# Linear attention and a bilinear feed-forward on one core: every matrix product as plain fp32 on four 32-column tiles

## The chip, the core and the metric

The kernel runs on one core of a Trainium2 chip. The core has five engines that run side by side and meet at semaphores: TensorE (PE in the profile; its weight loads are listed apart as PEld), VectorE (DVE), ScalarE (ACT), GpSimd (POOL) and SyncE (SP), whose queue starts most of the transfers. The metric is the device time of one execution in microseconds (us); lower is better.

## What is computed

A linear attention with a complex decay per channel, four batches by eight heads by 768 steps with 48 channels, and then a feed-forward of two products that are multiplied elementwise and a third product. Cut to what matters:

```
scale = np.minimum(mag, 0.999) / (mag + 1e-06)      # mag = |a_re + i a_im|
for t in range(S):                                  # S = 768
    S_re, S_im = (ar * S_re - ai * S_im + k_t v_t^T, ar * S_im + ai * S_re)
    y[:, :, t] = q_t @ S_re
x = y as (3072 tokens, 384)
out = ((x @ w_a) * (x @ w_b)) @ w_out               # d_model 384, d_ff 1536
```

Inputs, weights and result are fp32.

## The kernel before, in words

**Units.** The work is cut into 12 units: two pairs of batches, six chunks of 128 steps each. A unit has 256 tokens (two batches of 128, index `i`) and all eight heads. `prep(u)` makes a unit's decays and scaled queries and keys on DVE and ACT, `stack(u)` copies them into `stk` by DMA, `attn(u)` is the chunked attention, and the feed-forward of unit `u` runs while the attention of unit `u + 1` is made. The loop at the end goes over units `w` and, in each, over the 12 blocks `f` of 128 columns of d_ff: `gemm1` of block `f`, some pieces of `attn(w + 1)` (`slot`), then `gemm2` of the block two earlier (`LAG` is 2).

**Matrix products on PE.** Two sorts stand side by side. The feed-forward is made in fp32r, a reduced form of fp32 that is read in one pass, on all 128 columns of the array: weights, x and the product h are each held as a high part (rounded to fp32r) and a low part (what is left), and each product is made of three: high by high, low by high, high by low. `gemm1` (L549) makes for each of the two halves `m` (w_a and w_b) of a block 3 x 3 matmuls with 256 moving columns (`ab`); ACT and DVE then turn `ab` into `h_t`, `hh` and `hl` (L560 to L563: ACT copy, DVE product, ACT rounding, DVE difference). `gemm2` (L570) makes for each of two token halves three matmuls with 384 moving columns into `o`. The attention is in plain fp32: `scores` (L432, 128 moving columns), `transposes` of keys (L443, PE's transpose, 96 columns), `state` (L499, 48 or 96 moving columns) on all 128 or 96 columns, and `outputs` (L476, into `xp`), which alone is cut into tiles of 32 array columns: four matmuls, one for each quarter of the output's partitions, are issued one behind the other.

**Weights.** They lie in memory as 64-bit pairs. Three DVE operations (L140, L142, L144) turn a block's pairs into fp32 in a scratch tile; ACT rounds it (L148, high part), PE subtracts the high part from it (L153 in fp32, L154 in fp32r, times minus one with `nident`), and ACT copies out the low part (L155). Six blocks are done ahead of the first attention, six during unit 0. In the attention, x gets its low part in `residual` (L484 on DVE; L486 on PE and L489 on ACT for the first two units).

**What sets the order.** Each engine works its instructions off in program order; a scheduler places them by priority when the program is built (`high_priority` moves the evacuations of PSUM forward), and `issue_after` holds pieces of the attention behind a named matmul of the feed-forward.

Of the kernel before, what the change touches and what calls it, by code (L numbers as in the profile page):

```python
# [9 lines left out]
F32R = mybir.dt.float32r  # L10
# [42 lines left out]
CONV_ON_AB = 7  # L53
# [20 lines left out]
def tile_kernel(ctx: ExitStack, tc: tile.TileContext, a_d, qk_d, v_d, w_d, qn_d, kn_d, vn_d, an_d, out_d):  # L74
# [45 lines left out]
    nident = const.tile([128, 128], F32, name="nident")  # L120
    act.mul(out=nident.bitcast(F32R), in_=ident, mul=-1.0)
    w_t = {}
    raws = {}

    def r(ap):
        return ap.bitcast(F32R)

# [6 lines left out]
    def split_weights():  # L134
        for f in range(NF):
            for m, (c0, n) in enumerate(WPART):
# [12 lines left out]
                if f < CONV_ON_AB:  # L149
                    lp = ps_ab.tile([128, 512], F32, name="ab")  # L150
                else:
                    lp = ps_m.tile([128, 512], F32, name="pm")
                pe.matmul(out=lp[:, 0:n], lhsT=ident, rhs=t, start=True, stop=False)  # L153
                pe.matmul(out=lp[:, 0:n], lhsT=r(nident), rhs=r(hi), start=False, stop=True)  # L154
                act.copy(out=r(lo), in_=lp[:, 0:n])  # L155
# [255 lines left out]
    ff_last = [None, None]  # L411

    def attn(u, xh, xl):
# [10 lines left out]
        def scores(i, hg):  # L424
            qs, ks = cols(i)
            sp = ps_m.tile([128, 4, 128], F32, name="pm")
            for h4 in range(4):
                h = hg * 4 + h4
                with ExitStack() as behind:
                    if u >= GATE_FROM and not ams:  # L430
                        behind.enter_context(tc.issue_after(ff_last[0]))
                    pe.matmul(out=sp[:, h4], lhsT=stk[:, h, ks], rhs=stk[:, h, qs], start=True, stop=True)  # L432
# [6 lines left out]
        def transposes(i, hg):  # L439
            qs, ks = cols(i)  # L440
            tp = ps_m.tile([128, 512], F32, name="pm")
            for h4 in range(4):
                pe.transpose(out=tp[:, h4 * KS:(h4 + 1) * KS], in_=stk[0:KS, hg * 4 + h4, ks],  # L443
                             identity=ident[0:KS, 0:KS])
# [6 lines left out]
        def outputs(i, _):  # L451
# [17 lines left out]
            with tc.high_priority(offset=ATTN_FIRST):  # L469
# [8 lines left out]
                act.copy(out=r(xh[:, :, qs]), in_=xp)  # L478

        def residual(i, _):  # L480
            qs, ks = cols(i)
            if u > 1:
                with tc.high_priority(offset=ATTN_FIRST):
                    vec.tensor_tensor(out=r(xl[:, :, qs]), in0=xps[i], in1=xh[:, :, qs], op=ALU.subtract)  # L484
                return
            pe.matmul(out=xps[i], lhsT=r(nident), rhs=r(xh[:, :, qs]), start=False, stop=True,  # L486
                      skip_group_check=True)
            with tc.high_priority(offset=ATTN_FIRST):
                act.copy(out=r(xl[:, :, qs]), in_=xps[i])  # L489

        def state(i, hg):
# [4 lines left out]
            for h4 in range(4):  # L496
                h = hg * 4 + h4
                o = (h // 2) * VG + (h % 2) * (64 if own else 16)
                pe.matmul(out=kp[0:KS, h4 * n:(h4 + 1) * n], lhsT=kt_tiles[u][:, i, h * KS:(h + 1) * KS],  # L499
                          rhs=v_t[:, o:o + n], start=True, stop=True)  # L500
# [3 lines left out]
            with tc.high_priority(offset=ATTN_FIRST):  # L504
# [4 lines left out]
                if rescaled(c):  # L509
# [3 lines left out]
                 (outputs, 0, 0), (scores, 1, 0), (residual, 0, 0), (state, 0, 0), (scores, 1, 1),  # L513
                 (state, 0, 1), (transposes, 1, 0), (transposes, 1, 1), (outputs, 1, 0),
                 (state, 1, 0), (residual, 1, 0), (state, 1, 1)]
        if u >= KT_FROM:
            order = [(scores, 0, 0), (scores, 0, 1), (pause, 0, 0), (outputs, 0, 0), (scores, 1, 0),
                     (residual, 0, 0), (state, 0, 0), (scores, 1, 1), (state, 0, 1), (outputs, 1, 0),
                     (state, 1, 0), (residual, 1, 0), (state, 1, 1)]
        if u == 0:  # L520
            order = [(scores, 0, 0), (scores, 0, 1), (outputs, 0, 0), (scores, 1, 0), (scores, 1, 1),
                     (residual, 0, 0), (outputs, 1, 0), (transposes, 0, 0), (transposes, 0, 1),
                     (residual, 1, 0), (state, 0, 0), (state, 0, 1), (transposes, 1, 0), (transposes, 1, 1),
# [6 lines left out]
    def pieces(u):  # L530
        if u >= KT_FROM:
            return 9 if u % NCH + 1 == NCH else 13
        return 8 if u % NCH + 1 == NCH else 16

    def new_x():
        return (moe.tile([128, NJ, TOK], F32, name="xh"), moe.tile([128, NJ, TOK], F32, name="xl"))


    def w_ab(f, part, blk):
        m, b = divmod(blk, NJ)  # L540
        return w_t[f, m][:, part, b * 128:(b + 1) * 128]

    def gemm1(f, xh, xl, ps_ab=ps_ab, moe=moe, spare=None):
        ab = ps_ab.tile([128, 512], F32, name="ab")
        for m in range(2):
            n = 0
            for i in range(NJ):
                for part, xt in ((0, xh), (0, xl), (1, xh)):
                    ff_last[0] = pe.matmul(out=ab[:, m * TOK:(m + 1) * TOK],  # L549
                              lhsT=r(w_ab(f, part, m * NJ + i)),  # L550
                              rhs=r(xt[:, i, :]), start=n == 0, stop=n == 8).ins
                    n += 1
        if spare and f % 2:
            h_t = spare()[:, 0:TOK]
        else:
            h_t = moe.tile([128, TOK], F32, name="h_t", bufs=1)
        hh = moe.tile([128, TOK], F32, name="hh", bufs=HB)
        hl = moe.tile([128, TOK], F32, name="hl", bufs=HB)
# [286 lines left out]
```

## Time and profile before

| | |
|---|---|
| median of 3 runs | 684.1 us (683.79 to 685.3) |
| the profiled execution's own time | 683.28 us |
| its span, first to last instruction | 681.5 us |
| mean granted TensorE clock | 0.969 of full speed |
| busy: PE, PEld, DVE, ACT, POOL | 639.5, 603.5, 558.1, 334.9, 5.5 us |
| instructions: PE, DVE, ACT | 5778, 1283, 670 |
| moved by DMA | 63.14 MB, 93 GB/s |

The profile has one row for each group of equal instructions: line, engine, operation, tile written and read, shape, count, then the busy time and the mean duration of one. A matmul's form reads as "rows*columns of the array", then what it streams. A plain fp32 matmul shows as two instructions, each with its own weight load (192 products of `scores` are 384 instructions); an fp32r matmul and PE's transpose as one. Matmuls overlap, so a duration in a row is a latency; what one costs in a stream is the distance from its start to the next one's. In the view of the slices, a digit is the busy share of a fortieth of the span in tenths, and PEclk the granted clock in tenths.

### The profile page before, as it was taken

What the parts mean: (1) busy time and instruction counts of PE and PEld (TensorE: products, weight loads), DVE (VectorE), ACT (ScalarE), POOL (GpSimd) and SP (SyncE); (2) the same over time, 40 slices, a digit from 0 to 9 for tenths busy, and PEclk for the clock granted to TensorE, in tenths of its full rate; (3) what the DMA queues carried; (4) which work ended last, traced back from release to release, by engine and by line L of the source; (5) the groups of instructions that cost most, each with busy time, mean ns of one, the idle gap of its engine ahead of it and who ended that gap; (6) DMA issues with size and microseconds to landing.
All of it is one profiled execution on the core that took longest, in us unless ns stands there. A gap on an engine that the chain in (4) does not pass through costs nothing.

```text
span 681.5 us, 14237 instructions
## 1 busy us (share of the span) xinstructions
PE 639.5 (94%) x5778; PEld 603.5 (89%) x5778; DVE 558.1 (82%) x1283; ACT 334.9 (49%) x670; POOL 5.5 (1%) x11
## 2 busy tenths in 40 slices
PE   3547899999999999999999999999999999999996
PEld 1214789999999999999999999999999999999996
DVE  6999899998989989989899899899899898433221
ACT  7347665734545446255363464664573573222321
POOL 3000000000000000000000000000000000000000
PEclk9576899999999999999999999999999999999998
DMA  8983300512415115033151151601511500400000
GB/s 286 395 317 94 120 1 12 176 51 64 124 39 149 57 48 183 16 116 108 29 164 47 38 154 48 166 25 49 148 42 62 154 24 15 119 12 2 24 1 27
DMA packets 52120, 63.14 MB, mean 93 GB/s; under 512 B 28624, under 2 KB 32208, under 8 KB 52048
## 3 DMA queue, kind: packets, MB, share of 16 engines
q1 hardware_dynamic: 48592, 57.45, 28.0%
q10 hardware_dynamic: 3456, 4.72, 1.9%
q8 instruction: 47, 0.77, 0.5%
q14 instruction: 25, 0.20, 0.1%
HBM read 38.54 MB, written 4.72 MB: 63 GB/s over the span
## 4 chain that ended last, share of the span: by engine, by line
PE 53%; DVE 32%; ACT 7%; DMA 3%; issue 3%; SPq 2%; ACTq 0%; DVEq 0%
PE ab L549 27%; PE o L570 13%; PE xp L476 4%; PE pm L432 4%; DVE a_t L300 3%; PE pm L499 3%; DVE qk L320 3%; DVE pr L238 2%; DVE hl L563 2%; DVE am L435 2%; ACT kt L408 2%; DVE z L305 1%; DVE o_sb L142 1%; DVE h_t L561 1%; DVE z L244 1%
## 5 line engine op out<-in xcount | busy, mean ns | idle before, releaser
L549 PE MATMUL ab<-xh,w 128*128 128x256 f32 x1728 | 339.2, 285 | 0.0
L549 PEld LDWEIGHTS ab<-xh,w 128*128 128x128 f32 x1728 | 276.1, 188 | 2.8 <-issue 2.0
L549 PE MATMUL ab<-xl,w 128*128 128x256 f32 x864 | 244.3, 283 | 0.0
L549 PEld LDWEIGHTS ab<-xl,w 128*128 128x128 f32 x864 | 162.8, 188 | 0.5
L570 PE MATMUL o<-w,hh 128*128 128x384 f32 x576 | 153.7, 346 | 0.4 <-ACT o_sb L709 0.4
L570 PEld LDWEIGHTS o<-w,hh 128*128 128x128 f32 x576 | 97.3, 188 | 1.5 <-ACT o_sb L709 0.6
L570 PE MATMUL o<-w,hl 128*128 128x384 f32 x288 | 97.3, 338 | 0.0
L560 ACT COPY h_t<-ab 128x256 f32<-128x256 f32 x75 | 27.6, 368 | 67.5 <-PE ab L549 65.4
L153 PE MATMUL ab<-o_sb,ident 128*128 128x384 f32 x42 | 28.0, 766 | 30.0 <-DVE o_sb L144 30.0
L432 PE MATMUL pm<-stk 128*128 128x128 f32 x384 | 54.6, 281 | 0.6 <-DMA stk<-qk 0.5
L570 PEld LDWEIGHTS o<-w,hl 128*128 128x128 f32 x288 | 54.1, 188 | 0.0
L432 PEld LDWEIGHTS pm<-stk 128*128 128x128 f32 x384 | 50.1, 194 | 4.4 <-issue 2.2
L560 ACT COPY o_sb<-ab 128x256 f32<-128x256 f32 x66 | 24.3, 369 | 59.7 <-PE ab L549 59.1
L561 DVE TENSOR_TENSOR h_t<-ab,h_t 128x256 f32<-128x256 f32 x75 | 31.5, 420 | 26.0 <-ACT h_t L560 25.9
L562 ACT CAST hh<-h_t 128x256 fp32r<-128x256 f32 x75 | 30.1, 402 | 44.2 <-DVE h_t L561 44.1
L561 DVE TENSOR_TENSOR o_sb<-ab,o_sb 128x256 f32<-128x256 f32 x66 | 27.7, 420 | 29.0 <-ACT o_sb L560 29.0
L238 DVE TENSOR_TENSOR pr<-z 128x384 f32<-128x384 f32 (+1 forms) x91 | 47.2, 525 | 2.0
L562 ACT CAST hh<-o_sb 128x256 fp32r<-128x256 f32 x66 | 26.6, 403 | 45.1 <-DVE o_sb L561 44.9
L300 DVE TENSOR_TENSOR a_t<-z,b_t 128x768 f32<-128x768 f32 x48 | 45.1, 954 | 0.0
L153 PEld LDWEIGHTS ab<-o_sb,ident 128*128 128x128 f32 x42 | 9.5, 267 | 39.4 <-DVE o_sb L144 29.6
L320 DVE TENSOR_TENSOR qk<-qk,z 128x768 f32<-128x768 f32 (+1 forms) x34 | 43.5, 1279 | 0.2
L476 PE MATMUL xp<-am,v_t 128*32 128x128 f32 x768 | 37.7, 281 | 2.9 <-DVE am L435 2.8
(117 smaller groups left out, 897.8 us busy)
## 6 DMA issues: line engine op xcount, KB each, us to landing
w<-in_dram SPq DMA_DIRECT2D x36, 384.0 KB, 7.8
qk<-in_dram SPq DMA_DIRECT2D x12, 768.0 KB, 4.8
stk<-qk SPq DMA_DIRECT2D x48, 192.0 KB, 3.3
a_t<-in_dram SPq DMA_DIRECT2D x11, 768.0 KB, 4.5
stk<-qk SPq DMA_DIRECT2D x24, 192.8 KB, 3.3
out_dram<-o_sb ACTq DMA_DIRECT2D x24, 192.0 KB, 1.9
v_t<-in_dram SPq DMA_DIRECT2D x24, 128.0 KB, 2.6
v_t<-in_dram SPq DMA_DIRECT2D x24, 96.0 KB, 3.0
```

What stands on the lines that cost most here:

```text
L153: pe.matmul(out=lp[:, 0:n], lhsT=ident, rhs=t, start=True, stop=False)
L238: vec.tensor_tensor(out=pr[:, :, :, o:o + n], in0=view(zz, W + at_(i) + 2 * o, [[W, 2], [-W, 2], [2, n]]), in1=tok(slice(1, 3), i - 1, o, ...
L300: vec.tensor_tensor(out=pz[:, s].rearrange("p (j b e) -> p j b e", j=SUB // 2, e=2), in0=zb[:, 1 + s], in1=view(bb, (1 + k - s) * NB, [[0, ...
L320: vec.tensor_tensor(out=qk4[:, :, k, x0:x1], in0=qk4[:, :, 1, x0:x1], in1=z[:, k].rearrange("p (j t) -> p j t", j=NJ).unsqueeze(2).broadca ...
L432: pe.matmul(out=sp[:, h4], lhsT=stk[:, h, ks], rhs=stk[:, h, qs], start=True, stop=True)
L476: run = pe.matmul(out=xp[qd * 32:(qd + 1) * 32, ti], lhsT=l, rhs=rr, start=st, stop=sp_, tile_position=(0, qd * 32), skip_group_check=True ...
L499: pe.matmul(out=kp[0:KS, h4 * n:(h4 + 1) * n], lhsT=kt_tiles[u][:, i, h * KS:(h + 1) * KS], rhs=v_t[:, o:o + n], start=True, stop=True)
L549: ff_last[0] = pe.matmul(out=ab[:, m * TOK:(m + 1) * TOK], lhsT=r(w_ab(f, part, m * NJ + i)), rhs=r(xt[:, i, :]), start=n == 0, stop=n == ...
L560: act.copy(out=h_t, in_=ab[:, 0:TOK])
L561: vec.tensor_tensor(out=h_t, in0=ab[:, TOK:2 * TOK], in1=h_t, op=ALU.mult)
L562: ff_last[1] = act.copy(out=r(hh), in_=h_t).ins
L570: ff_last[0] = pe.matmul(out=os_[tt][:, 0:DM], lhsT=r(ht[:, ts]), rhs=r(w_t[f, 2][:, part, :]), start=(f == 0 and n == 0), stop=(f == NF - ...
```

## The change

All matrix products go through one helper, `tiled`, or through `outputs`, whose matmuls are in that form already. The helper cuts the stationary operand into quarters of 32 columns and issues one plain fp32 matmul for each quarter, the last quarter first. The high and low parts of weights, x and h are gone, with what made them: per weight block two ACT copies and two PE matmuls (the third DVE operation now writes the fp32 weight over the front half of the block's own pairs), `residual`, ACT's rounding and DVE's difference of h. Scores, transposes (now a product with the identity) and state go through `tiled` as well. `gemm1` takes 3 products of 256 columns for each half instead of 9, `gemm2` one of 384 columns for each token half instead of 3.

```diff
+    def tiled(out, lhsT, rhs, start=True, stop=True):
+        for qd in reversed(range(lhsT.shape[-1] // 32)):
+            q = slice(qd * 32, (qd + 1) * 32)
+            ff_last[0] = pe.matmul(out=out[q], lhsT=lhsT[:, q], rhs=rhs, start=start, stop=stop,
+                                   tile_position=(0, qd * 32), skip_group_check=True).ins
...
-                vec.scalar_tensor_tensor(out=tu, in0=raw[:, :, 1], scalar=0xC0000000, in1=tu,
+                w = raw.rearrange("p c s -> p (c s)")[:, 0:n]
+                w_t[f, m] = w.bitcast(F32)
+                vec.scalar_tensor_tensor(out=w, in0=raw[:, :, 1], scalar=0xC0000000, in1=tu,
                                          op0=ALU.bitwise_and, op1=ALU.bitwise_or)
-                w_t[f, m] = wpool.tile([128, 2, n], F32, name=f"w{m}{f}")
-                hi, lo = w_t[f, m][:, 0], w_t[f, m][:, 1]
-                act.copy(out=r(hi), in_=t)
...
-                pe.matmul(out=lp[:, 0:n], lhsT=ident, rhs=t, start=True, stop=False)
-                pe.matmul(out=lp[:, 0:n], lhsT=r(nident), rhs=r(hi), start=False, stop=True)
-                act.copy(out=r(lo), in_=lp[:, 0:n])
...
-                    pe.matmul(out=sp[:, h4], lhsT=stk[:, h, ks], rhs=stk[:, h, qs], start=True, stop=True)
+                    tiled(sp[:, h4], stk[:, h, ks], stk[:, h, qs])
...
-                pe.transpose(out=tp[:, h4 * KS:(h4 + 1) * KS], in_=stk[0:KS, hg * 4 + h4, ks],
-                             identity=ident[0:KS, 0:KS])
+                tiled(tp[:, h4 * KS:(h4 + 1) * KS], stk[0:KS, hg * 4 + h4, ks], ident[0:KS, 0:KS])
...
-                act.copy(out=r(xh[:, :, qs]), in_=xp)
-
-        def residual(i, _):
...
+                act.copy(out=x_t[:, :, qs], in_=xp)
...
-                pe.matmul(out=kp[0:KS, h4 * n:(h4 + 1) * n], lhsT=kt_tiles[u][:, i, h * KS:(h + 1) * KS],
-                          rhs=v_t[:, o:o + n], start=True, stop=True)
+                tiled(kp[0:KS, h4 * n:(h4 + 1) * n], kt_tiles[u][:, i, h * KS:(h + 1) * KS], v_t[:, o:o + n])
...
         for m in range(2):
-            n = 0
             for i in range(NJ):
-                for part, xt in ((0, xh), (0, xl), (1, xh)):
-                    ff_last[0] = pe.matmul(out=ab[:, m * TOK:(m + 1) * TOK],
-                              lhsT=r(w_ab(f, part, m * NJ + i)),
-                              rhs=r(xt[:, i, :]), start=n == 0, stop=n == 8).ins
-                    n += 1
...
+                tiled(ab[:, m * TOK:(m + 1) * TOK], w_t[f, m][:, i * 128:(i + 1) * 128], x_t[:, i, :],
+                      i == 0, i == NJ - 1)
+        a_sb = moe.tile([128, TOK], F32, name="a_sb")
+        h_t = moe.tile([128, TOK], F32, name="h_t", bufs=HB)
         with tc.high_priority(offset=MOE_FIRST):
-            act.copy(out=h_t, in_=ab[:, 0:TOK])
-            vec.tensor_tensor(out=h_t, in0=ab[:, TOK:2 * TOK], in1=h_t, op=ALU.mult)
-            ff_last[1] = act.copy(out=r(hh), in_=h_t).ins
-            vec.tensor_tensor(out=r(hl), in0=h_t, in1=hh, op=ALU.subtract)
-        return hh, hl
+            ff_last[1] = act.copy(out=a_sb, in_=ab[:, 0:TOK]).ins
+            vec.tensor_tensor(out=h_t, in0=ab[:, TOK:2 * TOK], in1=a_sb, op=ALU.mult)
+        return h_t
...
-            ts = slice(tt * 128, (tt + 1) * 128)
-            for n, (ht, part) in enumerate(((hh, 0), (hh, 1), (hl, 0))):
-                ff_last[0] = pe.matmul(out=os_[tt][:, 0:DM], lhsT=r(ht[:, ts]), rhs=r(w_t[f, 2][:, part, :]),
-                          start=(f == 0 and n == 0), stop=(f == NF - 1 and n == 2)).ins
+            tiled(os_[tt][:, 0:DM], h_t[:, tt * 128:(tt + 1) * 128], w_t[f, 2], f == 0, f == NF - 1)
```

The lines that drop the `residual` entries from the order of the attention's pieces, adapt the count of pieces and rename arguments are left out of the diff.

What this does to PE's instructions shows in the built programs, where a matmul is one row whatever its passes; a row has the line, the operation, the tile written and the tiles read (with numbers where several exist), the output's shape and a count. First the steady state of the feed-forward, in the middle of unit 2. Before, the second half of `gemm1` of one block and `gemm2` of the block two earlier read:

```order
L549 MATMUL ab<-xh,w_438 128x256
L549 MATMUL ab<-xl,w_438 128x256
L549 MATMUL ab<-xh,w_438 128x256 x2
L549 MATMUL ab<-xl,w_438 128x256
L549 MATMUL ab<-xh,w_438 128x256 x2
L549 MATMUL ab<-xl,w_438 128x256
L549 MATMUL ab<-xh,w_438 128x256
L570 MATMUL o_2258<-w_388,hh 128x384 x2
L570 MATMUL o_2258<-w_388,hl 128x384
L570 MATMUL o_2259<-w_388,hh 128x384 x2
L570 MATMUL o_2259<-w_388,hl 128x384
```

In the changed program, PE's rows at the same place hold both halves of a block, its `gemm2`, and the first half of the next block; every row is now written by the helper (L123):

```order
L123 MATMUL ab<-x_t,w_146 32x256 x12
L123 MATMUL ab<-x_t,w_148 32x256 x12
L123 MATMUL o_2526<-w_130,h_t 32x384 x4
L123 MATMUL o_2527<-w_130,h_t 32x384 x4
L123 MATMUL ab<-x_t,w_152 32x256 x12
```

Nine full-width matmuls of a half have become twelve of a quarter's width, and three of a token half have become four; the sequence of blocks is the same.

Second, a place in unit 2 where pieces of the next unit's attention stand between the blocks: scores (`pm<-stk`), state (`pm<-v_t,kt`) and transposes (`pm<-ident,stk`). Before:

```order
L432 MATMUL pm<-stk 128x128 x4
L499 MATMUL pm<-v_t,kt 96x48 x4
L570 MATMUL o_2258<-w_894,hh 128x384 x2
L570 MATMUL o_2258<-w_894,hl 128x384
L570 MATMUL o_2259<-w_894,hh 128x384 x2
L570 MATMUL o_2259<-w_894,hl 128x384
L443 MATMUL pm<-ident,stk 128x96 x8
```

And PE's rows in the changed program around the same pieces:

```order
L123 MATMUL pm<-v_t,kt 32x48 x12
L123 MATMUL pm<-stk 32x128 x16
L123 MATMUL ab<-x_t,w_188 32x256 x12
L123 MATMUL ab<-x_t,w_190 32x256 x12
L123 MATMUL pm<-v_t,kt 32x48 x12
L123 MATMUL pm<-ident,stk 32x96 x16
L123 MATMUL o_2526<-w_180,h_t 32x384 x4
L123 MATMUL o_2527<-w_180,h_t 32x384 x4
L123 MATMUL pm<-ident,stk 32x96 x16
```

Each of four products is now four matmuls (scores, transposes) or three (state), and pieces of the attention stand between the same blocks of the feed-forward or one block further on.

Third, the start of PE's program. Before, it begins with the products that make the weights' low parts:

```order
L153 MATMUL ab<-o_sb,ident 128x384 x2
L154 MATMUL ab<-w_338,nident 128x384
L153 MATMUL ab<-o_sb,ident 128x384
L154 MATMUL ab<-w_348,nident 128x384
L154 MATMUL ab<-w_358,nident 128x384
```

Now it begins with the attention of unit 0:

```order
L123 MATMUL pm<-stk 32x128 x48
L466 MATMUL xp<-am,v_t 32x128 x16
L123 MATMUL pm<-stk 32x128 x16
L123 MATMUL pm<-ident,stk 32x96 x20
L466 MATMUL xp<-am,v_t 32x128 x16
```

All 36 pairs of L153 and L154 are gone, from the start and from among the blocks of unit 0.

More of the change, by code (lines that the diff above doesn't have):

```diff
@@ L117, in tile_kernel @@
         nc.gpsimd.memset(u_t, 0.0)
-    nident = const.tile([128, 128], F32, name="nident")
-    act.mul(out=nident.bitcast(F32R), in_=ident, mul=-1.0)
+    ff_last = [None, None]
+    def tiled(out, lhsT, rhs, start=True, stop=True):
[3 more added lines that the diff above has]
+                                   tile_position=(0, qd * 32), skip_group_check=True).ins
     w_t = {}
     raws = {}
-    def r(ap):
-        return ap.bitcast(F32R)
     def load_weights(f):
@@ L409, in place_keys, with attn @@
             yield
-    ff_last = [None, None]
-    def attn(u, xh, xl):
+    def attn(u, x_t):
         c = u % NCH
@@ L477, in outputs @@
                                             tile_position=(0, qd * 32), skip_group_check=True).ins
-                act.copy(out=r(xh[:, :, qs]), in_=xp)
-        def residual(i, _):
[L481 to L489, printed above, removed]
+                act.copy(out=x_t[:, :, qs], in_=xp)
         def state(i, hg):
@@ L512, in attn @@
         order = [(scores, 0, 0), (scores, 0, 1), (transposes, 0, 0), (transposes, 0, 1),
[L513 removed]
+                 (outputs, 0, 0), (scores, 1, 0), (state, 0, 0), (scores, 1, 1),
                  (state, 0, 1), (transposes, 1, 0), (transposes, 1, 1), (outputs, 1, 0),
[L515 removed]
+                 (state, 1, 0), (state, 1, 1)]
         if u >= KT_FROM:
             order = [(scores, 0, 0), (scores, 0, 1), (pause, 0, 0), (outputs, 0, 0), (scores, 1, 0),
[L518 to L519 removed]
+                     (state, 0, 0), (scores, 1, 1), (state, 0, 1), (outputs, 1, 0),
+                     (state, 1, 0), (state, 1, 1)]
         if u == 0:
             order = [(scores, 0, 0), (scores, 0, 1), (outputs, 0, 0), (scores, 1, 0), (scores, 1, 1),
[L522 to L523 removed]
+                     (outputs, 1, 0), (transposes, 0, 0), (transposes, 0, 1),
+                     (state, 0, 0), (state, 0, 1), (transposes, 1, 0), (transposes, 1, 1),
                      (state, 1, 0), (state, 1, 1)]
@@ L531, in pieces @@
         if u >= KT_FROM:
-            return 9 if u % NCH + 1 == NCH else 13
-        return 8 if u % NCH + 1 == NCH else 16
+            return 7 if u % NCH + 1 == NCH else 11
+        return 6 if u % NCH + 1 == NCH else 14
     def new_x():
[L536 to L543, printed above, removed]
+        return moe.tile([128, NJ, TOK], F32, name="x_t")
@@ L544, in gemm1 @@
+    def gemm1(f, x_t, ps_ab=ps_ab, moe=moe):
         ab = ps_ab.tile([128, 512], F32, name="ab")
         for m in range(2):
-            n = 0
             for i in range(NJ):
-                for part, xt in ((0, xh), (0, xl), (1, xh)):
-                    ff_last[0] = pe.matmul(out=ab[:, m * TOK:(m + 1) * TOK],
-                              lhsT=r(w_ab(f, part, m * NJ + i)),
-                              rhs=r(xt[:, i, :]), start=n == 0, stop=n == 8).ins
-                    n += 1
[L553 to L556, printed above, removed]
@@ L655, in feed_forward @@
                                                in_=rows[r0:r0 + n, bass.ds(c * C, C)])
-                xh = p1.tile([128, NJ, TOK], F32, name="xh")
-                xl = p1.tile([128, NJ, TOK], F32, name="xl")
-                act.copy(out=r(xh), in_=xt)
-                vec.tensor_tensor(out=r(xl), in0=xt, in1=xh, op=ALU.subtract)
                 os_ = [pp.tile([128, 512], F32, name=f"o{t}", bufs=1) for t in range(2)]
                 for f in range(NF):
-                    gemm2(f, *gemm1(f, xh, xl, pp, p1), os_)
+                    gemm2(f, gemm1(f, xt, pp, p1), os_)
                 for tt in range(2):
@@ L697, in tile_kernel @@
     x_cur = new_x()
-    for _ in attn(0, *x_cur):
+    for _ in attn(0, x_cur):
         drain(p1, P1_A)
@@ L702, in second @@
     def second():
-        w2, f2, hh, hl, os2 = pend.pop(0)
-        gemm2(f2, hh, hl, os2)
+        w2, f2, h_t, os2 = pend.pop(0)
+        gemm2(f2, h_t, os2)
         if f2 == NF - 1:
@@ L710, in second @@
                 act.dma_start(out=out_d[w2, tt], in_=o_sb)
-    def spare_h(w, f):
-        if w > 0:
-            return lambda: moe.tile([128, DM], F32, name="o_sb", bufs=O_BUFS)
-        if f <= ATTN_AT[0]:
-            return lambda: kvp.tile([128, 2, H * KS], F32, name="kt", bufs=1)[:, 0]
     def attn_at(w):
@@ L724, in tile_kernel @@
         x_nxt = None if last else new_x()
-        at = None if last else attn(w + 1, *x_nxt)
+        at = None if last else attn(w + 1, x_nxt)
         if not last:
@@ L749, in tile_kernel @@
                     pgen = prep(2)
[L750 removed]
+            pend.append((w, f, gemm1(f, x_cur), os_))
             slot()
@@ L781, in tile_kernel @@
     for tt in range(2):
-        for w2, f2, hh, hl, os2 in pend:
-            gemm2(f2, hh, hl, os2, (tt,))
+        for w2, f2, h_t, os2 in pend:
+            gemm2(f2, h_t, os2, (tt,))
         o_sb = moe.tile([128, DM], F32, name="o_sb", bufs=O_BUFS)
```

11 lines of the change are left out of this document (1 added, 10 removed).

## The prediction

> **What bounds the kernel now.** I read the page first: busy times, the slices, the chain that ended last.
>
> ```profile
> span 681.5 us, 14237 instructions
> PE 639.5 (94%) x5778; PEld 603.5 (89%) x5778; DVE 558.1 (82%) x1283; ACT 334.9 (49%) x670; POOL 5.5 (1%) x11
> ...
> PE   3547899999999999999999999999999999999996
> ...
> DVE  6999899998989989989899899899899898433221
> ...
> PEclk9576899999999999999999999999999999999998
> ...
> PE 53%; DVE 32%; ACT 7%; DMA 3%; issue 3%; SPq 2%; ACTq 0%; DVEq 0%
> ```
>
> PE is full from the fifth slice (about 75 us) to the end, at the full granted clock; DVE is full before that and nearly full behind it. So about 75 us of start belong to DVE, and some 600 us to PE. A PE that is full for hundreds of us is paced by the distance from start to start. The chain in order of time gives it for one block of the feed-forward:
>
> ```profile
> 207.39 2.15 PE ab L549 x18
> 209.54 1.06 PE o L570 x6
> 210.60 2.15 PE ab L549 x18
> ```
>
> (Start, length, what.) One block takes 2.15 + 1.06 = 3.21 us: 0.119 us for each fp32r matmul of 256 columns, 0.176 for one of 384. 144 blocks are 462 us, two thirds of the span. The prediction hangs on what a block costs in tiles.
>
> **What a wave of four tiles costs.** The outputs of the attention have that form already. PE's timeline over one such stretch:
>
> ```profile
> 321.69 0.28 PE L549 MATMUL ab<-xh,w 128*128 128x256 f32 x1
> 321.90 0.43 PE L476 MATMUL xp<-am,v_t 128*32 128x128 f32 x8
> 322.14 0.40 PE L476 MATMUL xp<-stk,u 128*32 128x128 f32 x8
> ...
> 323.45 0.40 PE L476 MATMUL xp<-stk,u 128*32 128x128 f32 x8
> 323.78 0.62 PE L570 MATMUL o<-w,hh 128*128 128x384 f32 x2
> 324.24 0.34 PE L570 MATMUL o<-w,hl 128*128 128x384 f32 x1
> ```
>
> Each row is four tiles in two passes. From 322.14 to 323.45 are six rows: 1.31 / 6 = 0.218 us, so one wave (four tiles, one pass, 128 columns) takes 0.109 us. What more columns cost, the full-width fp32 products of the weight split show:
>
> ```profile
> 82.01 0.81 PE L153 MATMUL pm<-o_sb,ident 128*128 128x384 f32 x2
> 82.36 0.63 PE L154 MATMUL pm<-w,nident 128*128 128x384 f32 x1
> 82.83 0.81 PE L153 MATMUL pm<-o_sb,ident 128*128 128x384 f32 x2
> ```
>
> From 82.01 to 82.83 run two fp32 passes and one fp32r matmul of 384 columns: (0.82 - 0.176) / 2 = 0.322 us a pass. Between 128 and 384 columns a pass grows by (0.322 - 0.109) / 256 = 0.00083 us a column, so a wave of 256 columns takes 0.216 us. That the wave follows its columns, not its weight load, shows where the clock was halved:
>
> ```profile
> 69.92 1.94 PE xp L476 x32
> 74.51 1.08 PE xp L476 x32
> ...
> 69.92:71.41 1.49, 1.49 (x28) 1.39 (x32) 0.81 (x1) 0.00 (x0) 0.00 (x0) 0.50 0.86 334
> 74.51:75.28 0.77, 0.77 (x29) 0.77 (x32) 0.77 (x2) 0.22 (x2) 0.00 (x0) 1.00 0.90 327
> ...
> L476 PEld LDWEIGHTS xp<-am,v_t x768: 106/110/178, 69.9 to 620.8; 128*32 128x32 f32 x192
> L476 PE MATMUL xp<-am,v_t x768: 269/272/423, 69.9 to 620.9; 128*32 128x128 f32 x192
> ```
>
> (Chain; the same two stretches as windows, where 0.50 and 1.00 are the granted clock; minimum, median and maximum of one, in ns.) Eight waves less the last one's latency: (1.94 - 0.42) / 7 = 0.217 us at half clock, (1.08 - 0.27) / 7 = 0.115 at full. The wave doubles; the longest weight load is 0.178 us and would not fill it.
>
> **The change part by part**, against the profiled execution (683.28 us, 1.8 outside its span, and 0.1% under the median of 684.1).
>
> (A) *Feed-forward.* A block becomes 2 x 3 products of 256 columns in two passes, 12 waves of 0.216, and 2 products of 384, 4 waves of 0.322: 2.59 + 1.29 = 3.88 us for 3.21. 0.67 x 144 = **+96.5 us**. Bounds: the pure column cost without an overhead of 0.002 a wave gives 3.84 (+91), a wave in proportion to 0.109 gives 3.93 (+104).
>
> (B) *Weight split and start.* 36 pairs of L153 and L154 go. Those on the second PSUM pool stand among unit 0's blocks:
>
> ```profile
> L153 PE MATMUL pm<-o_sb,ident 128*128 128x384 f32 x30 | 12.6, 505 | 0.0
> L154 PE MATMUL pm<-w,nident 128*128 128x384 f32 x15 | 7.9, 535 | 0.0
> ```
>
> 30 x 0.322 + 15 x 0.176 = 12.3 us of a full PE. The earlier ones filled idle time. The start itself stays DVE's: its three operations a weight remain, only waits for ACT and PE fall out, 1 to 2 us; against that, PE now starts the attention out of idleness, at the halved clock that the window at 69.92 shows. In unit 0 DVE is full as well, so part of the 12.3 may come back as DVE's pace; DVE loses its `hl` there (0.42 us a block) and should keep up. I take **-12** (-16 to 0).
>
> (C, D) *Transposes and state.*
>
> ```profile
> 269.11 0.49 PE L443 MATMUL pm<-ident,stk 96*128 96x96 f32 x4
> ...
> 276.15 0.80 PE L499 MATMUL pm<-v_t,kt 128*96 128x48 f32 x8
> ...
> L432 PE MATMUL pm<-stk 128*128 128x128 f32 x384 | 54.6, 281 | 0.6 <-DMA stk<-qk 0.5
> L443 PE MATMUL pm<-ident,stk 96*128 96x96 f32 x96 | 12.5, 250 | 0.4 <-DVE am L435 0.4
> L499 PE MATMUL pm<-v_t,kt 128*96 128x48 f32 x256 | 25.8, 244 | 0.0
> L499 PE MATMUL pm<-v_t,kt 128*96 128x96 f32 x64 | 6.6, 251 | 0.0
> ```
>
> A transpose costs (0.49 - 0.25) / 3 = 0.08 us in one pass; it becomes two waves of 96 columns, 2 x 0.082: 96 x 0.084 = **+8** (with 0.109 a wave, +13; if short waves cost less, +5). A state product costs two passes of (0.80 - 0.25) / 7 = 0.079 to 0.085 (the pace of the transposes' 96 weight columns, not of 48 moving ones); it becomes two waves of 48 columns, 0.042 by columns, at most 0.109 if the tile's weight load paces it. I take 0.05, nearer to the column price, since weight loads hid behind waves at both clocks: 128 x (0.10 - 0.165) and 32 x 0.0 = **-8** (-10 to +9).
>
> (E) *Scores.* 192 products, 384 passes:
>
> ```profile
> 266.43 1.56 PE pm L432 x14
> ```
>
> 1.56 / 14 = 0.111 a pass against 0.109 a wave: **-1**. Four tiles side by side gain nothing where a pass is as long as its columns.
>
> (F) *Switches.* In the timeline above, the step into tiles took 0.21 us instead of 0.12, and counted back from 324.24 the first `gemm2` matmul began its work at 323.89, not 323.67: 0.31 us for each of 24 stretches, 7.4 us, which go when everything has one form. The h that `gemm2` waits for loses ACT's rounding and DVE's difference (0.4 us each, off the path while blocks are two behind). **-9** (-12 to 0).
>
> ACT loses 72 weight copies and 144 roundings, DVE the differences of h and x:
>
> ```profile
> L563 DVE TENSOR_TENSOR hl<-h_t,hh 128x256 fp32r<-128x256 f32 x75 | 31.4, 419 | 8.2 <-ACT hh L562 8.1
> L563 DVE TENSOR_TENSOR hl<-o_sb,hh 128x256 fp32r<-128x256 f32 x66 | 27.9, 422 | 7.6 <-ACT hh L562 7.4
> L484 DVE TENSOR_TENSOR xl<-xp,xh 128x384 fp32r<-128x384 f32 x20 | 11.0, 552 | 4.2 <-ACT xh L478 4.2
> ```
>
> DVE goes from 558 to about 487 us. That is worth nothing while PE is full, and is no new bound. DMA and its queues keep their work.
>
> Sum: 96.5 - 12 + 8 - 8 - 1 - 9 = +74.5; 683.3 + 74.5 = **758 us**.
>
> **The rivals.** *A faster wave (ends faster).* The mechanism: a pass in tiles costs what an fp32r matmul costs, because 0.109 at full clock was a tile's weight load (0.110) and not its columns. A block counts as 12 + 4 x 1.5 = 18 waves of 256 columns, so the turning point is 3.21 / 18 = 0.178 us; the forecast has 0.216. At 0.119 a block takes 2.14, 154 us less, with the other terms (-22) about 507 us, by then near DVE's 487. For it speaks that load and wave coincide at full clock; against it the doubling at half clock, L153's 0.322, and that a pass has a median of 272 ns in tiles and 281 at full width on the same columns. 4%. The Trainium skill (Perfetto Trace Analysis, section Engine Utilization) halves the array's output rate for FP32_LOW_HIGH, which read for a whole fp32 product gives this case; its page FP8 and Floating Point Precision (TensorE Precision Notes) counts four passes for true fp32, and the trace sides with that one: 2 x 0.322 is 3.7 times the fp32r matmul's 0.176.
>
> *Supply of instructions (slower).* A block has 16 waves x 4 tiles x 2 = 128 PE instructions, one each 30 ns; before it was 48 in 3.21 us, one each 67. Instructions that come slower than 30 ns pace every block; at 40 ns a block takes 5.1 us and the kernel about 936 (683 + 275 - 22).
>
> ```profile
> 133.35:143.35 10.00, 10.00 (x183) 9.07 (x183) 9.69 (x22) 5.43 (x10) 0.00 (x0) 1.00 0.28 86
> q8 instruction: 47, 0.77, 0.5%
> ```
>
> Against it: 10 us with 366 PE instructions, 27 ns each. But no row shows it for longer, and the fetched 0.77 MB more than double. 4%. The Trainium skill (TensorE: Matmul & The Clock Gate, Part 2, decode and dispatch) gives about 62 ns a matmul where the sequencer's own code decodes it; a block's 64 would take an estimated 3.97 us, 0.09 more, and the sum would be near 771. The 183 matmuls in 10 us are one each 55 ns, so the trace disagrees.
>
> *Clock or order (slower).* The granted clock falls below full under tiles alone (the longest such stretch so far is 1.9 us): at half clock some 600 us more. Or the change doesn't do what it says, the four tiles running one after another: a block of up to 15.5 us. Eight rows of 0.218 us against it. Together 3%.
>
> **How the numbers follow.** 0.89 for the forecast, 0.04 for the faster wave, 0.07 for the slower ones. The terms' own bounds reach from 742 (all low) to 808 (all high); not all fall on one side, and A's and D's weigh most. I take 744 to 787, in which I see 0.82 of the chance. A difference under 0.2% can't be told from none: slower 0.95, the same 0.01, faster 0.04.
>
> **What would show it.** In the chain, a block as 48 `ab` instructions over 2.59 us and 16 `o` over 1.29; waves 0.216 and 0.322 apart; PE's share of the chain well over 53%; the first `ab` near 77 us; DVE near 487 us busy, ACT near 240; state waves near 0.05. Wrong it would be if tiles of 256 columns start less than 0.178 us or clearly more than 0.216 apart, or if PEclk shows other than 9s.

## The result, and the profile after

The changed kernel takes **828.7 us** (median of 4 runs, 828.2 to 829.4) against 683.9 us for the kernel before on the same chip (4 runs, 683.3 to 685.3): a ratio of 1.211 (95% interval 1.209 to 1.214). It is slower, as forecast, but 71 us slower than the 758 forecast and 42 above the top of the range. The profiled execution took 828.5 us.

The page after: busy times, slices and the chain that ended last.

```profile
span 826.7 us, 30060 instructions
PE 700.1 (85%) x13890; PEld 525.2 (64%) x13890; DVE 507.1 (61%) x1119; ACT 250.4 (30%) x449; POOL 5.5 (1%) x11
...
PE   0007969996995996989989899999999999999997
...
DVE  6999999888897268249458222783983962111110
...
PEclk9999989998997997998999899999999999999999
...
DVE 48%; PE 33%; ACT 7%; DMA 6%; issue 3%; SPq 2%; DVEq 0%; ACTq 0%
```

Before, PE's row was 9s from the sixth slice on (an 8 in the fifth) and PE had 53% of the chain. Now there are 5s, 6s and 8s every third slice or so up to the middle, PEclk dips in the same places, and DVE has 48% of the chain although it is busy only 61% of the time. An engine that is mostly idle and yet carries the chain is late at particular places, not short of time.

The blocks themselves cost what was forecast. The chain in order of time, where it runs through PE:

```profile
615.42 1.50 PE o L123 x16
616.91 2.59 PE ab L123 x48
619.50 1.29 PE o L123 x16
```

48 `ab` instructions take 2.59 us and 16 of `o` 1.29, the figures of term A (the first `o` here, 1.50, starts out of a wait). From one wave to the next, the median distance of starts at full clock is 216 ns for 256 columns, 322 for 384, 109 for 128 and 82 for 96. The state's wave has three tiles, not four (96 columns of keys); it takes 43 ns at 48 columns. The 2 x 3 + 2 products of a block do take 3.88 us.

What is new are PE's waits (engine, line, what for; us in total, times, longest). In the kernel before, the largest are these:

```profile
PE ab L153 <- DVE o_sb L144: 30.0, 13, 9.5
PE xp L476 <- DVE am L435: 2.8, 3, 2.2
```

In the changed kernel:

```profile
PE pm L123 <- DMA stk<-qk: 67.0, 3, 60.1
PE pm L123 <- DVE am L426: 30.5, 7, 8.0
PE o L123 <- ACT o_sb L665: 8.1, 5, 3.3
PE o L123 <- DVE h_t L526: 4.7, 7, 0.9
```

The 60.1 us of the first row is the start, which PE before spent on the weight split and its waits for DVE. From the first `ab` (76.6 us) to the last matmul, pauses of PE longer than 0.3 us add up to 55.5 us in 25 places; in the kernel before to 1.1 us in 3. Most of it is `am` (L426), the masked copy of scores out of PSUM. PE's timeline at the longest of these waits, then DVE's over the same time:

```profile
313.64 1.94 PE L123 MATMUL pm<-stk 128*32 128x128 f32 x61
...
315.51 1.47 PE L123 MATMUL o<-w,h_t 128*32 128x384 f32 x15
324.98 2.99 PE L123 MATMUL pm<-ident,stk 96*32 96x96 f32 x64 [8.01 <-DVE am L426]
```

```profile
315.86 0.96 DVE L190 SCALAR_TENSOR_TENSOR sc<-a_t,sc 128x768 f32<-128x768 f32 x1
...
317.73 0.19 DVE L266 TENSOR_TENSOR pb<-tt,b_t 128x24 f32<-128x24 f32 x1
...
322.18 1.82 DVE L293 TENSOR_TENSOR a_t<-z,b_t 128x768 f32<-128x768 f32 x2
323.91 0.42 DVE L526 TENSOR_TENSOR h_t<-ab,a_sb 128x256 f32<-128x256 f32 x1
324.25 0.68 DVE L426 TENSOR_TENSOR am<-pm,mask 128x512 f32<-128x512 f32 x1
```

The scores, two groups, end at 314.8 and 315.7. The mask that empties the first group's PSUM tile runs at 324.25, because some thirty instructions, nearly all of a later unit's preparation, stand ahead of it in DVE's queue. The transposes want one of the two `pm` tiles and wait 8.01 us; the blocks behind them in PE's queue wait with them. And then the clock:

```profile
312.00:316.00 4.00, 4.00 (x108) 3.76 (x104) 3.93 (x9) 1.47 (x3) 0.00 (x0) 1.00 0.02 4
316.00:324.00 8.00, 0.97 (x14) 0.23 (x4) 7.55 (x28) 0.00 (x0) 0.00 (x0) 0.82 0.00 0
325.00:328.00 3.00, 3.00 (x68) 2.62 (x72) 3.00 (x4) 0.48 (x1) 0.00 (x0) 0.50 0.02 5
```

(Windows: length, then busy time of PE, PEld, DVE, ACT and POOL, then the granted clock.) PE is busy 0.97 of 8 us, DVE 7.55; when PE starts again its clock is 0.50. Seven such half-speed stretches begin in or just behind seven waits, 51 us in all; 35 of them lie outside the waits, and of these at most half, some 17 us, is lost. Together with the pauses that is about 73 us that PE stands or crawls. At the distances above its work from the first `ab` to the last matmul is about 664 us, and it took 744; the remaining 7 us were not traced.

### The profile page after: what moved, and what is told of

The parts are those of the page before. It is cut to its first block, busy times and chain, and to the rows that moved or that the text cites. A ratio compares the mean times of both kernels' runs of the same rounds, so it can differ in the third digit from the quotient of the medians.

```text
span 826.7 us, 30060 instructions
## 1 busy us (share of the span) xinstructions
PE 700.1 (85%) x13890; PEld 525.2 (64%) x13890; DVE 507.1 (61%) x1119; ACT 250.4 (30%) x449; POOL 5.5 (1%) x11
## 4 chain that ended last, share of the span: by engine, by line
DVE 48%; PE 33%; ACT 7%; DMA 6%; issue 3%; SPq 2%; DVEq 0%; ACTq 0%
PE ab L123 18%; PE o L123 9%; DVE pr L231 5%; DVE a_t L293 5%; PE pm L123 4%; DVE qk L313 3%; DVE z L237 3%; DVE z L298 2%; PE xp L466 2%; DVE h_t L526 2%; DMA a_t<-in_dram 2%; DVE pb L266 2%; DVE o_sb L143 2%; SPq L360 2%; DVE w L147 2%
## 5 line engine op out<-in xcount | busy, mean ns | idle before, releaser
L123 PE MATMUL ab<-x_t,w 128*32 128x256 f32 x6912 | 425.8, 386 | 2.0 <-ACT x_t L468 2.0
L123 PEld LDWEIGHTS ab<-x_t,w 128*32 128x32 f32 x6912 | 308.4, 112 | 90.5 <-issue 26.0
L123 PE MATMUL o<-w,h_t 128*32 128x384 f32 x2304 | 225.7, 489 | 13.0 <-ACT o_sb L665 8.1
L526 DVE TENSOR_TENSOR h_t<-ab,a_sb 128x256 f32<-128x256 f32 x144 | 60.2, 420 | 192.0 <-ACT a_sb L525 192.0
L123 PEld LDWEIGHTS o<-w,h_t 128*32 128x32 f32 x2304 | 101.6, 110 | 65.6 <-issue 26.1
L525 ACT COPY a_sb<-ab 128x256 f32<-128x256 f32 x144 | 52.4, 367 | 258.7 <-PE ab L123 242.2
L123 PE MATMUL pm<-stk 128*32 128x128 f32 x1536 | 56.6, 283 | 69.6 <-DMA stk<-qk 67.0
L123 PEld LDWEIGHTS pm<-stk 128*32 128x32 f32 x1536 | 46.5, 113 | 79.2 <-issue 63.0
L123 PE MATMUL pm<-ident,stk 96*32 96x96 f32 x768 | 27.4, 287 | 30.3 <-DVE am L426 28.1
L123 PEld LDWEIGHTS pm<-ident,stk 96*32 96x32 f32 x768 | 23.4, 130 | 36.0 <-DVE am L426 31.8
L426 DVE TENSOR_TENSOR am<-pm,mask 128x512 f32<-128x512 f32 x48 | 32.7, 687 | 16.2 <-PE pm L123 15.5
L466 PEld LDWEIGHTS xp<-am,v_t 128*32 128x32 f32 x768 | 26.3, 110 | 12.2 <-ACT a_sb L525 5.4
L466 PE MATMUL xp<-stk,u 128*32 128x128 f32 x640 | 34.0, 273 | 0.0
L123 PEld LDWEIGHTS pm<-v_t,kt 128*32 128x32 f32 x960 | 21.8, 110 | 11.7 <-issue 6.7
```

Of the source, the lines that this page charges most:

```text
L123: ff_last[0] = pe.matmul(out=out[q], lhsT=lhsT[:, q], rhs=rhs, start=start, stop=stop, tile_position=(0, qd * 32), skip_group_check=True).ins
L426: vec.tensor_tensor(out=am, in0=sp, in1=mask[:].unsqueeze(1).broadcast_to([128, 4, 128]), op=ALU.mult)
L466: run = pe.matmul(out=xp[qd * 32:(qd + 1) * 32, ti], lhsT=l, rhs=rr, start=st, stop=sp_, tile_position=(0, qd * 32), skip_group_check=True ...
L525: ff_last[1] = act.copy(out=a_sb, in_=ab[:, 0:TOK]).ins
L526: vec.tensor_tensor(out=h_t, in0=ab[:, TOK:2 * TOK], in1=a_sb, op=ALU.mult)
```

## The experiments

Three theories. **T1**: the loop deals DVE more preparation per block than a block now lasts, so DVE is late whatever its order. **T2**: the tiles themselves (their waves, their instructions, their switches) stall PE. **T3**: the scheduler, which sees the tiled program, has put DVE's instructions in another order, and the masks stand too late in it. Each was timed once, beside the kernel before on the same chip (683.0 to 683.9 us), where no interval is given. "Pauses" are PE's, over 0.3 us, between the first `ab` and the last matmul.

**Full width in place of tiles** (`wide`).

```diff
-        for qd in reversed(range(lhsT.shape[-1] // 32)):
-            q = slice(qd * 32, (qd + 1) * 32)
-            ff_last[0] = pe.matmul(out=out[q], lhsT=lhsT[:, q], rhs=rhs, start=start, stop=stop,
-                                   tile_position=(0, qd * 32), skip_group_check=True).ins
+        ff_last[0] = pe.matmul(out=out, lhsT=lhsT, rhs=rhs, start=start, stop=stop).ins
```

> The changed kernel with every product that went through the helper issued once at full width, still plain fp32, instead of as four tiles (outputs keep their tiles). Theory 1 (DVE late: in the first two thirds of a unit the loop hands DVE more work per block than a block lasts, the mask product of the scores stands behind it, PE waits, and its clock halves after the wait): a pass costs the same at full width (0.216 and 0.322), so the waits stay in kind; 790 to 840 us, with PE gaps of several us before transposes or scores in most of units 1 to 5. Theory 2 (the tiles themselves: four times the matmuls, and their supply or issue costs PE the 70 us): the gaps and the half clock go, 760 to 775 us. Theory 3 (the scheduler orders DVE badly because it counts four tiles as four full matmuls): also 760 to 775, with another DVE order.

792.3 us, pauses 12.0 us. A pass of 256 columns costs the same 0.216 us at full width, so four tiles side by side cost per column what one plain fp32 product costs; that speaks against T2. The time lies in T1's range, above the 760 to 775 of T2 and T3, but T1's waits of several us in most units did not show: the longest pause is 3.3 us. The edit also changed DVE's order, so it can't tell T1 from T3.

**Preparation dealt more evenly** (`even`): smaller portions for each block, queued behind the block's own h product.

```diff
-            yield 440 + (next(sg, 0) if i > 3 else 0)
+            yield 900 + (next(sg, 0) if i > 3 else 0)
...
+            yield 450
...
-            vec.tensor_tensor(out=h_t, in0=ab[:, TOK:2 * TOK], in1=a_sb, op=ALU.mult)
+            h_ins.append(vec.tensor_tensor(out=h_t, in0=ab[:, TOK:2 * TOK], in1=a_sb, op=ALU.mult).ins)
...
-                drain(pgen, 2400)
+                with tc.issue_after(h_ins[-1]):
+                    drain(pgen, 2450)
```

> The changed kernel with DVE's preparation of decays dealt out evenly: its steps carry about their measured lengths, 2450 a block, and each block's share is held behind the h product of that block; all of PE's products as in the changed kernel. Theory 1: PE's waits behind the mask products shrink to under 20 us in all after the start, hardly any half clock after 80 us, 750 to 785 us. Theory 2: nothing that paces tiles has changed, 815 to 835. Theory 3: as theory 1, since the order is forced.

783.5 us, pauses 23.7. TensorE's work is as in the changed kernel, and 45 us are gone, so the tiles by themselves are not what costs the 71 us: T2 falls as the whole cause. T1 and T3 both allow it.

**The two halves of the change** (`ff_tiles`: the changed kernel with scores, transposes and state at full width; `attn_tiles`: the reverse edit on the kernel before, only these three in tiles and the feed-forward in fp32r).

```diff
-                    tiled(sp[:, h4], stk[:, h, ks], stk[:, h, qs])
+                    pe.matmul(out=sp[:, h4], lhsT=stk[:, h, ks], rhs=stk[:, h, qs], start=True, stop=True)
```

> Only the feed-forward in tiles of plain fp32; scores, transposes and state at full width as before the change. Theory 1: the blocks are as slow as in the changed kernel and DVE is dealt the same, so the waits stay: 800 to 840 us. Theory 2: four fifths of the tile instructions remain, 810 to 830. Theory 3: three fifths of the misjudged attention is gone, 780 to 820.

> The kernel before with only scores, transposes and state in tiles; the feed-forward keeps fp32r with high and low parts. The terms C, D and E of the prediction are +8, -8 and -1 us; against them stand some 110 more stretches with a switch of form at 0.2 to 0.3 us each, 22 to 34 us. Theory 1 (blocks of 3.21 us, DVE as full as before): 700 to 725 us, without gaps of several us. Theory 2: the same, since few tile instructions run. Theory 3: gaps of several us before transposes appear here too, 730 to 760.

829.3 us with pauses of 32.0, and 719.3 with 12.5. The halves don't add up: the attention's tiles alone cost 35 us on the kernel before, and taking them away from the changed kernel gains nothing. Both edits reorder DVE too, so a sum of parts can't be read from them. Both times lie outside T3's ranges (780 to 820 and 730 to 760) and inside T1's. T3 gave those ranges because it took the scheduler to count four tiles as four full matmuls; no run here bears that part out.

**DVE's order by itself.** The 1119 DVE instructions of the changed kernel were chained, each behind its predecessor, in an order taken from another program (the same instructions there, found by source line and count; `DVE_ORDER` is the list of their 1119 places). The chain is of issue alone, it adds no wait for a result. It does not hold the other engines: the scheduler places their instructions anew around it.

```diff
+    dve = [i for i in nc.cur_bb.bb.instructions if i.engine == cnt_i.engine]
+    for a, b in zip(DVE_ORDER, DVE_ORDER[1:]):
+        tc.add_manual_dep(dve[b], dve[a].name,
+                          mybir.DependencyInfo(mybir.DependencyClass.NoSync, mybir.DependencyReason.DATA),
+                          reason="dve order")
```

`tiles_border` is the changed kernel in the order of the kernel before, `wide_torder` the run `wide` in the changed kernel's order, `wide_border` the run `wide` in the order of the kernel before.

> The changed kernel, with its 1119 VectorE instructions queued in the order in which the kernel before has the same instructions (its 164 differences hl and xl left out); the work of all engines is unchanged. T3 (the stalls come from the place of the masks am in VectorE's queue): 745 to 780 us, gaps of TensorE under 20 us in sum where the changed kernel has 55. T1 (VectorE is late whatever its order, since each block is dealt more VectorE work than a block lasts): 805 to 830. T2 (the tiles themselves): 815 to 830.

> The kernel of the run wide (one full-width fp32 product in place of four tiles, 792.3 us, gaps of TensorE 12 us), with its VectorE instructions queued in the order of the changed kernel. No tiles but those of the outputs. T3 (order): the stalls come back, 815 to 845 us, gaps over 35 us. T1: about as wide, 785 to 800. T2 (tiles): as wide, 788 to 796.

> The kernel of the run wide with its VectorE instructions in the order of the kernel before. With tiles_border it compares tiles and full width at one and the same VectorE order. T3: gaps under 20 us, 760 to 795 us, and a difference to tiles_border of 5 to 25 us that is the switches of form and the outputs alone. T2: tiles_border is slower than this by 30 us or more. T1: 785 to 800.

| DVE's order | in tiles | at full width |
|---|---|---|
| of the kernel before | 764.9 us, pauses 11.0 | 775.8 us, pauses 2.0 |
| of `wide` | 798.8, 33.7 (below) | 792.3, 12.0 |
| of the changed kernel | 828.7, 55.5 | 817.0, 26.6 |

T3 is shown in both directions, for DVE's order and what follows it: the same TensorE work falls by 64 us with the old order, and the full-width kernel, which has no tiles but the outputs', rises by 25 with the new one (its pauses, 26.6, stay below the 35 that T3 expected). T1 falls: the amount of DVE work is equal in every row. At the old order the tiles are even 11 us better than full width, and the state's products alone make up as much: 25.1 us at full width, 13.9 in tiles.

What else moved with the chain can be read from the traces of the changed kernel and of `tiles_border`, by counting the blocks that stand ahead of an instruction in its own engine's queue. PE's scores and outputs keep their block to within 1.3 (0.1 in the mean), ACT's copies of `kt`, `x_t` and `o_sb` to within 2. ACT's part of the preparation comes later with DVE's, its `a_t` by 7.5 blocks in the mean and 15 at most. So what the chain undoes is preparation that runs ahead, on both engines. PE's waits for ACT's copies are part of the price, 15.7 us in the changed kernel and 1.8 in `tiles_border`; the shares of the two engines' orders were not parted.

The page and PE's waits of `tiles_border`:

```profile
span 763.2 us, 30050 instructions
PE 682.9 (89%) x13890; PEld 557.4 (73%) x13890; DVE 509.3 (67%) x1119; ACT 252.5 (33%) x449; POOL 5.5 (1%) x11
...
PE   0006996999999999999999999999999999999997
...
PE 74%; DVE 18%; ACT 3%; DMA 2%; SPq 1%; issue 1%; ACTq 0%; DVEq 0%
```

```profile
PE pm L171 <- DMA stk<-qk: 69.9, 7, 60.6
PE xp L514 <- DVE am L474: 1.5, 3, 0.9
PE pm L171 <- DVE am L474: 1.4, 3, 0.9
```

PE is full again and has 74% of the chain; waits for `am` on the `pm` tiles are 1.4 us instead of 30.5 (line numbers are shifted by the list of the order). Blocks now follow each other without a break:

```profile
325.39 2.59 PE ab L171 x48
327.99 1.29 PE o L171 x16
329.27 2.59 PE ab L171 x48
331.87 1.29 PE o L171 x16
```

What differs in the two orders can be counted. How many DVE instructions other than masks, h products and weight split (nearly all of them preparation) stand ahead of a unit's first mask, and how many h products (one a block):

| first mask of | order before: preparation, h | order of `wide` | changed kernel |
|---|---|---|---|
| attention 2 | 228, 21 | 253, 21 | 281, 21 |
| attention 3 | 301, 33 | 351, 32 | 399, 33 |
| attention 4 | 366, 43 | 440, 43 | 460, 43 |

At the same block, the changed program has done up to 98 preparation instructions more: a unit's preparation is some 70 of them, so it is up to more than a whole unit ahead, and the masks stand behind it. From the end of its scores to its start a mask waits 110.7 us in sum over the 48 masks in the changed kernel (the worst 8.5 to 10.1 us, just those at 186, 256 and 317 us where PE pauses) and 52.0 in `tiles_border`.

**That result timed** (`border_timed`, the same kernel).

> The run tiles_border once more, timed in three rounds beside the kernel before. It measures what the change costs with VectorE's order held: T3 762 to 768 us, a ratio of 1.115 to 1.125; T1 and T2 hold no different number for a repetition.

765.9 us (764.0 to 767.5), a ratio of 1.119 (1.115 to 1.123).

**Only the masks moved** (`am_moved`): the chain again, now with the changed kernel's own order in the list, but each mask ahead of what began after its scores had ended. `am_moved2` takes the same step again from the trace of `am_moved`; only the list differs.

> The changed kernel with its own VectorE order but for the 48 masks am: each is queued ahead of the instructions that began, in the changed kernel's trace, after its scores had ended (26 of them move, over 155 instructions in all; the largest moves are those of the masks that ran 6 to 10 us after their scores). If the masks behind the preparation are what stops TensorE (T3 in its narrow form): the stalls near 186, 256, 317 and 453 us go, some 28 us of gaps and about half as much again of halved clock, 775 to 800 us. If the rest of VectorE's order matters as much (h, the state): 800 to 822. T1: the stalls only move, 820 to 835.

> The run am_moved with the same step taken once more from its own trace: 16 masks that ran after their scores had ended while VectorE began other work are moved ahead of it (50 instructions passed in all; those 8.5, 5.6 and 11.3 us late are the large ones). If the masks' place is the whole cause: 765 to 785 us, gaps under 20. If the rest of VectorE's order, the products h and the preparation's own end (which later steps wait for), holds a part of its own: 790 to 810, with gaps at other releasers than am.

807.5 and 803.4 us: the narrow forecast missed both times, and the wider one, in which the rest of the order matters too, held. PE's waits for masks fall from 32.5 us (30.5 on `pm`, 2.0 on `xp`) to 4.9, though two masks still start 9.3 and 10.5 us behind their scores; other waits have come. The larger ones in `am_moved2`:

```profile
PE o L171 <- DVE h_t L574: 18.3, 17, 3.0
PE pm L171 <- DVE u L532: 4.7, 3, 2.3
PE o L171 <- ACT o_sb L713: 4.3, 2, 2.7
PE xp L514 <- DVE am L474: 3.2, 4, 1.3
```

Now h products and state updates are late too. The masks are where the order shows first, and moving them gives 25 of the 64 us. That the rest comes from the same preparation, ahead of everything else that empties PSUM, fits these waits and the 64 us of the whole order; it was not tried by itself.

**The order of `wide` on tiles** (`tiles_worder`).

> The changed kernel with its VectorE instructions in the order of the run wide, whose source differs from the changed kernel's in tiled alone. It splits the order's cost: what the four tiles add to it when the order is made, and what the rest of the edit does. If VectorE's order sets the time whatever the form: near wide_border's distance to wide (16 us) above tiles_border, 775 to 795 us, with wide's small gaps (10 to 20 us). If tiles stall by themselves as well: over 800.

798.8 us, pauses 33.7: between the two expectations in time, and with more pauses than the 10 to 20 of the first. The step from the kernel before's order to that of `wide` costs 34 us on tiles and 16.5 at full width, the step on to the changed kernel's order 30 and 25. `wide` differs from the changed kernel in the helper `tiled` alone, so that second step is what the four tiles do to the scheduler's order; the first comes with the rest of the edit. One and the same late order costs more in tiles than at full width, by 17 and by 5 us. That share belongs to form and order together, and why it does was not traced.

**The split's TensorE work put back** (`b_back`), on `tiles_border`: for the 15 weights that are split among unit 0's blocks, two plain products that nobody reads.

```diff
+                if f >= 7:
+                    lp = ps_m.tile([128, 512], F32, name="pm")
+                    pe.matmul(out=lp[:, 0:n], lhsT=ident, rhs=w_t[f, m], start=True, stop=True)
+                    pe.matmul(out=lp[:, 0:104], lhsT=ident, rhs=w_t[f, m][:, 0:104], start=True, stop=True)
```

> The run tiles_border with the weight split's TensorE work put back among unit 0's blocks: for 15 weights one plain fp32 product of 384 columns and one of 104 at full width, 15 x (0.644 + 0.18) = 12.4 us, nobody reads them. If what the removed split work gave comes back as the wait at 117 us (7.2 us, and half of 6.8 us of halved clock behind it), the wait shrinks to under 2 us and the time stays within 762 to 768 us. If the split work was worth its 12 us: 774 to 779.

777.5 us, 11.6 more than `border_timed`: the removed work was worth its 12 us. The wait of unit 1's first scores, and the half clock behind it, did go, but the time rose all the same; shorter waits stand in its place (pauses 7.6 us in sum, 10.4 in `border_timed`). In `tiles_border` and in `b_back` the first scores of unit 1 stand so:

```profile
124.68 0.66 PE L171 MATMUL pm<-stk 128*32 128x128 f32 x8 [7.21 <-DMA stk<-qk]
```

```profile
136.49 0.88 PE L199 MATMUL pm<-w,ident 128*128 128x384 f32 x2 [0.26 <-DVE w L195]
...
137.50 1.30 PE L171 MATMUL pm<-stk 128*32 128x128 f32 x40
```

With more work on PE the scores start 13 us later, and DVE, whose h products wait for the blocks, idles 10.9 us instead of 4.5 between 77 and 117 us. It looks as if in unit 0 the two engines take turns; no further run tests that.

## Why the prediction was wrong

**The step that failed** is the sentence on DVE: "DVE goes from 558 to about 487 us. That is worth nothing while PE is full, and is no new bound." It takes DVE's order as given and asks only for its sum. The busy time is 507 us, far below the span, and DVE holds PE up all the same, since the program that the scheduler makes of the changed source has the preparation up to 98 instructions further ahead of the masks. The three places of the program that were looked at ahead of the prediction are all PE's; DVE's order, on which "worth nothing" hung, is none of them. Among the rivals, "clock or order" had 3% and thought of four tiles one after another and of a lower clock under tiles, not of an evacuation that is queued too late and of the clock that falls behind it.

**The other steps**, measured in `tiles_border`, where DVE's order is the one that the sum assumed. PE's time from the first `ab` to the last matmul, each stretch up to the next start put to the operation that opens it (waits within it included):

| term | forecast | measured |
|---|---|---|
| A, feed-forward blocks at their price | +96.5 | +96.4 (2.59 + 1.29 us a block) |
| F, what `ab` and `o` cost beyond that price | -9 | -2.0 (14.2 before, 12.2 after) |
| B, weight split | -12 | -12.0 |
| C, transposes | +8 | +8.0 |
| D, state | -8 | -11.0 |
| E, scores | -1 | +6.6 |
| outputs (with `residual` on PE) | 0 | -2.3 |
| start and end | in B and F | -1.8 |
| sum | +74.5 | +82 |

- *A* was right to a tenth: a wave costs its columns, 0.216 and 0.322 us; the faster wave and the supply of instructions (a block's 128 instructions in 3.88 us, the same in long stretches) both fell.
- *F* holds the one long pause that is left, 7.21 us at 117 us, and up to 2.4 lost at half clock behind it; without these 9.6 the blocks are within 3 us of their bare price, so the borders between unlike products did cost some 11.6, more than forecast. The 0.31 us a stretch of tiles is borne out (last section). What the forecast did not see is that the first fp32r matmul behind a plain fp32 product at full width (scores, state, split) or behind a transpose takes 0.08 us more as well: 8.3 us at 103 places in the kernel before.
- *B* came in full, by the table and by `b_back`. The caution that part of it may come back "as DVE's pace" is only half right: the pause of 7 us is there, but the removed work is worth its 12 us beside it.
- *D*: the wave of 48 columns takes 42 ns, the column price that the prediction had as its lower bound, and not the 0.05 taken: 128 x (0.084 - 0.165) = -10.4. The size was off, not the mechanism.
- *E*: a wave takes 109 ns as forecast; the 6.6 hold four short pauses of 0.3 to 0.9 us between 181 and 195 us and 1 us at half clock; the rest was not traced.
- Of the signs named, the first `ab` (76.6 for 77), ACT (250 for 240) and the waves of the feed-forward came out. DVE is busy 507 us, not 487: its durations add up to 67 us less (629 before, 563 after), but the page counts overlapping ones once, and that falls by only 51. PE's share of the chain (33%, not over 53%) and PEclk's 7s and 8s say what is wrong: the forecast asked for these two rows, and both spoke against it.

So 765.9 - 758 = 8 us of the miss are small terms, 63 are the order: some 44 us of pauses and, by the traces, at most 15 of halved clock; the other 4 were not traced.

Left open: by what rule the scheduler moves the preparation ahead when a product is four instructions. That the order changes with `tiled` alone is shown; why was not tried. Open too is why the same order costs more in tiles. No version here beats the kernel before.

## What to carry to other kernels

An edit that changes how many instructions one engine has can reorder another engine that the edit does not touch; read the new order of every engine that empties what the bound engine fills, and count what stands ahead of the evacuations. To price a change apart from its order, chain the engine's instructions in the old order: here that turned a miss of 71 us into one of 8. It holds one engine alone, so compare the others' queues as well. And plain fp32 in 32-column tiles gains next to nothing over plain fp32 at full width where products fill the array and move at least as many columns as they load.

## What the runs showed of the hardware

- Pauses of PE cost more than their length. Over the traces of the changed kernel and the 12 runs, all 20 pauses above 3.5 us, 13 of 14 between 2.5 and 3.5, 7 of 12 between 2.0 and 2.5 and 3 of 11 between 1.5 and 2.0 have a stretch at half clock that begins in them or within 3.5 us behind them, mostly 3.4 or 6.8 us long, at most 10.2; of 32 between 1.0 and 1.5 us, one has. The Trainium skill (TensorE: Matmul & The Clock Gate, Part 1) gives a window of about 3.4 us after which an idle PE drops to half rate, and as much of work to come back. The stretches of 3.4 and its multiples agree; the pauses below 3.4 us are shorter than the rule asks for.
- Four tiles of one plain fp32 pass take what one full-width pass of as many moving columns takes (216 ns at 256 columns in `wide` and in the changed kernel, 322 and 323 at 384, 109 and 112 at 128). Where fewer columns move, tiles are quicker: the state's wave of three tiles takes 42 ns at 48 columns, against 85 a pass at full width in `wide`, and a wave of transposes 82 against 112.
- Changing between full width and tiles costs about 0.31 us a stretch. In the kernel before and in `attn_tiles` the median step from an fp32r matmul into tiles is 0.21 us instead of 0.12, the step from the end of a wave of 128 columns to a full-width matmul 0.20 instead of 0.09 to the next wave, and the first full-width matmul behind takes 0.11 more. In `attn_tiles`, where only the attention went into tiles, this is a smaller part: the blocks' `ab` and `o`, the same instructions as before, take 20 us more from first to last, and some 13 of these are waits.
